# Maxout FFN behind cross attention on one core: transposes spread over the SyncE queue, deferred G copies, a last tile in two halves

## The chip, the core and the metric

The kernel runs on one core of a Trainium2 chip. The core has five engines with an instruction queue each: TensorE (PE, the matmuls; PEld are its weight loads), VectorE (DVE), ScalarE (ACT), GpSimd (POOL) and SyncE (SP, which here only issues DMAs). Instructions of one engine run in the order in which they were issued; engines wait for each other through semaphores. Matmuls write to PSUM, from which VectorE and ScalarE copy the results. The metric is the time of one execution on the device in microseconds (us), as a median over executions.

## What is computed

For each of 8 batches b and 8 heads h there are 512 rows x and 32 rows of state, 64 wide. Both read from each other by softmax attention, the results are put behind one another (544 rows for each batch, 4352 in all, the heads side by side to a width of 512), and a maxout FFN follows:

```python
scores = scale * np.matmul(x, state.transpose(0, 1, 3, 2))
a = np.exp(scores); a /= a.sum(-1, keepdims=True) + 1e-09     # over the 32 states
xread = np.matmul(a, state)
scores2 = scale * np.matmul(state, x.transpose(0, 1, 3, 2))
a2 = np.exp(scores2); a2 /= a2.sum(-1, keepdims=True) + 1e-09 # over the 512 rows
sread = np.matmul(a2, x)
t = np.concatenate([xread, sread], axis=2)                    # then (4352, 512)
h = np.maximum(np.maximum(t @ w1, t @ w2), t @ w3)            # d_ff = 768
out = h @ w_out
```

(The reference subtracts the row maximum before each exp.) Inputs and output are float32; the kernel computes in bf16 with float32 accumulation.

## The kernel before

**Algebra.** xread times w1, w2 or w3 is never computed by way of xread. `g_cols(b, ms)` multiplies the states of batch b with 128 columns of each of the three weights and so gives G, 256 rows (8 heads by 32 states) by 384 columns for each block m of 128 columns; `x_maxout(b, m)` multiplies the transposed softmax weights aT with G. d_ff = 768 makes six blocks m (NM = 6), each with 6 matmuls of 512 columns (three weights, two halves of the 256 states).

**One maxout (lines 264 to 279).** Three PSUM tiles `pw` are filled. ScalarE copies the first to `t0` in SBUF (line 275). If a copy is on the list `copies_due`, it is issued to ScalarE right behind that (line 277). VectorE takes the maximum of t0 and the second pw (line 278), and of that and the third (line 279), which gives one block of `ht`. The PSUM tag "pw" has four buffers, shared by pw, the output tiles `po`, the sread tile `psr` and the tiles of TensorE's transposes; a matmul that needs a buffer waits until the reader of what was in it before is done.

**G (lines 240 to 261).** Each block m is a PSUM tile `pg` of the tag "two", which has two buffers, also used by `scores`. The copy to G in SBUF is done by ScalarE: at once, or, where `defer` is True for this block, from `copies_due` inside the next maxout. `g_cols` first issues what is still on the list.

**For each batch.** `x_transpose` (TensorE) or `x_transpose_dma` (a DMA transpose on SP, line 163) gives xT, in two buffers; `scores` multiplies xT with the states and ScalarE takes exp into `e`; `softmax` sums, inverts (VectorE) and scales to `a` (GpSimd from batch 2 on); `a_transpose` or `a_transpose_dma` (SP, line 208) gives aT. `sread(b)` multiplies e with x, divides, and puts a small DMA transpose of the result (`sr`, 128 by 128, bf16, 32 KB) on the list `late` (line 230). `late_transposes()` issues what is on that list to SP. Its results, `ats`, are read only by `s_maxout`, in the last batch. `ffn_out(b, j)` multiplies 128 rows of ht with w_out (6 matmuls of 512 columns), ScalarE copies the 512 columns to `osb`, and every second tile they are stored.

**Order.** The program is unrolled and its order is written by hand. Lines 325 to 398 are a prologue: loads of x, states and weights (float32 to bf16, by GpSimd's DMA queue, lines 70 and 95), batches 0 and 1 interleaved, and the start of batch 2. Then batches b = 2 to 7 run in a loop (lines 401 to 428) of six `x_maxout(b, m)`, with other work in a slot behind each: after m = 0 the xT transpose of batch b+2 and the scores of n = b+1; then softmax, g_cols of b; after m = 2 the aT transpose of n; sread of n; after m = 4 `g_cols(n, (0, 1))`; after m = 5 `late_transposes`. `ffn_out(b-1, j)` stands behind m = 1, 2, 4, 5, in the last two cases ahead of the rest of its slot. In the last batch `s_maxout(m)` takes the place of the next batch's work. Lines 429 to 434 are the end: output tiles of batch 7 and of the sread rows, the last one with `split=True`.

Of the sread transposes, those of batches 0 to 3 are all issued at the first `late_transposes`, at the end of b = 2.

Of the kernel before, what the change touches and what calls it, by code (L numbers as in the profile page):

```python
# [8 lines left out]
F32 = mybir.dt.float32  # L9
# [6 lines left out]
def kernel(  # L16
# [14 lines left out]
    nc = tc.nc  # L31

    B, H, S, D = x.shape
    _, _, Ns, _ = state.shape
    HD = H * D
    SP = S + Ns
    T = B * SP
    d_model, d_ff = moe_w1.shape
# [3 lines left out]
    J = 4  # L42
    HS = H // 2
    NM = d_ff // 128
# [6 lines left out]
    work = ctx.enter_context(tc.tile_pool(name="work", bufs=2))  # L51
    pp = ctx.enter_context(tc.tile_pool(name="pp", bufs=2, space=bass.MemoryType.PSUM))
    ctx.enter_context(tc.manual_schedule())
    dve, act, pool = nc.vector.tensor_copy, nc.scalar.copy, nc.gpsimd.tensor_copy
# [34 lines left out]
    wout_sb = wpool.tile([128, NM, d_model], BF16, name="wout")  # L89
# [25 lines left out]
    def keep_busy(n):  # L115
        p = pp.tile([128, 1024], F32, tag="two", name="idle")
        for _ in range(n):
            nc.tensor.matmul(p[:, 0:512], zero[:, 0:128], zero, start=True, stop=True)  # L118


    def bd(b, h):
        return bds[b // 2][:, b % 2, h]
# [21 lines left out]
    xT, e, a, aT, G, ht, osb = {}, {}, {}, {}, {}, {}, {}  # L144

    def new(d, b, shape, name, bufs=2):
        d[b] = work.tile(shape, BF16, tag=name, bufs=bufs, name=name)
# [13 lines left out]
    def x_transpose_dma(b):  # L161
        new(xT, b, [128, H, 2, 128], "xT")
        nc.sync.dma_start_transpose(out=xT[b].rearrange("p h j t -> p (h j) t"), in_=x_sb[b][:, 0:XW])

    def scores(b, g0, g1):
        n = g1 - g0
        if g0 == 0:
            new(e, b, [128, J, 2, HS, Ns], "e")
        if n == 2:
            p = pp.tile([128, J, n, HS, Ns], F32, tag="two", name="ps")  # L170
        else:
            p = pp.tile([128, J, n, HS, Ns], F32, tag="pw", bufs=4, name="psh")
        for jj in range(2):
            for g in range(g0, g1):
                for s in range(HS):
                    h = 2 * s + g
                    nc.tensor.matmul(  # L177
                        p[:, 2 * jj:2 * jj + 2, g - g0, s, :], xT[b][:, h, jj, :],
                        bd(b, h).rearrange("p c n -> p (c n)"),
                        start=(g == g0 and s == 0 and (n == 2 or jj == 0)),  # L180
                        stop=(g == g1 - 1 and s == HS - 1), skip_group_check=True)
        nc.scalar.activation(out=e[b][:, :, g0:g1], in_=p, func=AF.Exp, scale=scale)  # L182

    def softmax(b, g0, g1, mul):
        n = g1 - g0
        if g0 == 0:
            new(a, b, [128, J, 2, HS, Ns], "a")
        den = work.tile([128, J, n, HS], F32, tag=f"den{n}", name="den")
        nc.vector.reduce_sum(out=den, in_=e[b][:, :, g0:g1], axis=AX.X)  # L189
        rden = work.tile([128, J, n, HS], F32, tag=f"rden{n}", name="rden")  # L190
        nc.vector.reciprocal(out=rden, in_=den)  # L191
        mul(  # L192
            out=a[b][:, :, g0:g1].rearrange("p j g s n -> p j (g s) n"),
            in0=e[b][:, :, g0:g1].rearrange("p j g s n -> p j (g s) n"),
            in1=rden.rearrange("p j g s -> p j (g s)").unsqueeze(3).to_broadcast((128, J, n * HS, Ns)))
# [40 lines left out]
    def flush_copies():  # L236
        while copies_due:
            copies_due.pop(0)()

    def g_cols(b, ms, copies=(nc.scalar.copy, nc.scalar.copy), defer=(False, False)):  # L240

        flush_copies()
        for m, copy, wait in zip(ms, copies, defer):
            if m == 0:
                new(G, b, [128, 2, NM * 384], "G", bufs=3)
            w, f = w_cols(m)
            p = pp.tile([128, 2, 512], F32, tag="two", name="pg")
            for s in range(HS):
                for g in range(2):
                    nc.tensor.matmul(  # L250
                        p[32 * s:32 * s + 32, g, 0:384].rearrange("p (i f) -> p i f", i=3),
                        bd(b, 2 * s + g)[64 * g:64 * g + 64, g, :], w[64 * g:64 * g + 64, s, :, f],
                        start=True, stop=True, tile_position=(64 * g, 32 * s))

            def place(m=m, p=p, copy=copy):
                copy(out=G[b][:, :, m * 384:(m + 1) * 384], in_=p[:, :, 0:384])  # L256

            if wait:
                copies_due.append(place)
            else:  # L260
                place()
# [19 lines left out]
    def x_maxout(b, m):  # L281
        maxout(b, m, 512,
               lambda i, k: G[b][:, k, m * 384 + i * 128:m * 384 + i * 128 + 128],
               lambda k: aT[b][:, :, k, :], 2)
# [6 lines left out]
    def ffn_out(b, j, split=False):  # L291
        if j == 0:
            osb[b] = work.tile([128, J, d_model], F32, tag="osb", name="osb")
        p = pp.tile([128, d_model], F32, tag="pw", bufs=4, name="po")
        for m in range(NM):
            nc.tensor.matmul(p, ht[b][:, m, j * 128:(j + 1) * 128], wout_sb[:, m, :],  # L296
                             start=(m == 0), stop=(m == NM - 1))
        o = osb[b]
        if split:
            halves = [work.tile([128, d_model // 2], F32, tag=f"oh{k}", bufs=1, name="oh") for k in range(2)]  # L300
            rows = out[b * SP:b * SP + S, :].rearrange("(p j) f -> p j f", j=J)[:, j, :]
            act(out=halves[0], in_=p[:, 0:256])
            nc.scalar.dma_start(out=rows[:, 0:256], in_=halves[0])
            dve(out=halves[1], in_=p[:, 256:512])
            nc.sync.dma_start(out=rows[:, 256:512], in_=halves[1])
            return
        act(out=o[:, j, :], in_=p)  # L307
        if b == "s":
            for k in range(4 * j, 4 * j + 4):
                r0 = k * SP + S  # L310
                (nc.sync if k % 4 < 2 else nc.gpsimd).dma_start(
                    out=out[r0:r0 + Ns, :], in_=o[32 * (k % 4):32 * (k % 4) + 32, j, :])
            return
        j0 = j if b == B - 1 and j >= 2 else j - 1
        if j == 1 or j == 3 or j0 == j:
            (nc.sync if b == B - 1 else nc.gpsimd).dma_start(  # L316
                out=out[b * SP:b * SP + S, :].rearrange("(p j) f -> p j f", j=J)[:, j0:j + 1, :],
                in_=o[:, j0:j + 1, :])


    def late_transposes():
        while late:
            late.pop(0)()
# [3 lines left out]
    states(0, act)  # L327
    for k in range(1, B // 2):
        nc.vector.memset(bds[k], 0.0)
    keep_busy(4)  # L330
    dve(out=x0_sb[0], in_=x0_f)
    x_transpose(0, 0, dve)
    x_transpose(0, 1, dve)
# [29 lines left out]
    sread(1)  # L363
    a_transpose(1, 0, act)
    a_transpose(1, 1, dve)
    g_cols(0, (2, 3))
    x_maxout(1, 0)
    x_maxout(0, 2)
    g_cols(1, (1, 2), defer=(False, True))
# [7 lines left out]
    x_maxout(0, 4)  # L377
    g_cols(1, (3, 4), defer=(False, True))
    x_maxout(1, 2)
    x_maxout(0, 5)  # L380
    scores(2, 0, 2)
    g_cols(1, (5,))
    x_maxout(1, 3)
    softmax(2, 0, 2, nc.gpsimd.tensor_mul)
    x_transpose_dma(3)
    ffn_out(0, 0)
    x_maxout(1, 4)
    g_cols(2, (0, 1))
    ffn_out(0, 1)
    load_x(4)  # L390
    for k in range(2, B // 2):
# [4 lines left out]
    sread(2)  # L396
    ffn_out(0, 2)
    ffn_out(0, 3)


    for b in range(2, B):
        n = b + 1
        slots = [[] for _ in range(NM)]
        if n < B:
            if n + 1 < B:
                slots[0].append(lambda: x_transpose_dma(n + 1))
            slots[0].append(lambda: scores(n, 0, 2))
            slots[1].append(lambda: softmax(n, 0, 2, nc.gpsimd.tensor_mul))
            slots[2].append(lambda: a_transpose_dma(n))
            if n % 2 and n + 1 < B:  # L410
                slots[2].append(lambda: states((n + 1) // 2, pool))
            slots[5].append(late_transposes)
            if n + 2 < B:
                slots[0].append(lambda: load_x(n + 2))
        else:
            for m in range(NM):
                slots[m].append(lambda m=m: s_maxout(m))
        slots[1].append(lambda: g_cols(b, (2, 3)))
        slots[2].append(lambda: g_cols(b, (4, 5)))
        if n < B:  # L420
            slots[3].append(lambda: sread(n))
            slots[4].append(lambda: g_cols(n, (0, 1)))
        for j, m in enumerate((1, 2, 4, 5)):
            slots[m].insert(0 if m > 2 else len(slots[m]), lambda j=j: ffn_out(b - 1, j))
        for m in range(NM):
            x_maxout(b, m)
            for f in slots[m]:
                f()
# [36 lines left out]
```

## Time and profile before

| | |
|---|---|
| median of 13 executions | 163.71 us (163.02 to 167.65) |
| the profiled execution | 163.06 us |
| its span, first to last instruction | 161.2 us |
| TensorE matmuls, busy | 148.6 us, 92% of the span |
| ScalarE, VectorE, GpSimd, busy | 96.9, 94.4, 51.0 us |
| GpSimd's DMA queue, SP's hardware queue | 49.2% and 22.6% of 16 DMA engines |
| granted TensorE clock | 1.00 |

The profile is of one execution, and times in it count from the first instruction. A row of the timeline has start, length, engine, line of the kernel, operation, what it writes and reads (out<-in), shapes and, behind an x, how many instructions were merged in it; in brackets the idle time of that engine before it and what ended it. A "q" behind an engine (SPq) means its queue: a DMA row there is the time that the queue took to issue the DMA, and it lands later. A matmul's length includes its way through the array, so that rows of unhindered matmuls overlap: six of 512 columns show 1.46, but the next ones start 1.29 to 1.31 after the first. A few matmul records are missing (x5 for six), and their time is not a wait.

### The profile page before, as it was taken

Reading aid. Unit: us, or ns where it says so; the run is one execution under the profiler, and the core shown is the slowest. Engines: PE = TensorE matmul, PEld = TensorE weight load, DVE = VectorE, ACT = ScalarE, POOL = GpSimd, SP = SyncE. Lnnn points to the kernel's source line nnn. Section 1 sums busy time; section 2 is a strip of 40 time slices with the busy share of each in tenths; the row PEclk is TensorE's granted clock in tenths of the full one; section 3 lists DMA queues with packets and bytes.
Section 4 is the critical chain, followed back from the end, with each engine's and each line's share of the span. In section 5 each row is a group of like instructions: output and inputs, shape, how many; then the busy total and the mean of one; then the engine's idle time right before and its main releaser. Section 6 shows DMA issues by size and latency. Waiting matters only on the chain.

```text
span 161.2 us, 3542 instructions
## 1 busy us (share of the span) xinstructions
PE 148.6 (92%) x1410; PEld 69.5 (43%) x1425; DVE 94.4 (59%) x161; ACT 96.9 (60%) x156; POOL 51.0 (32%) x72
## 2 busy tenths in 40 slices
PE   6775889999999999999799999999999999999990
PEld 2342433543554344443344344344434475566440
DVE  4788548586727665766366736673767484475201
ACT  3364577976748736974578287827782737633340
POOL 8859981000842417160204061411050100100140
PEclk9999999999999999999999999999999999999999
DMA  4999999959199993899995968070307030030374
GB/s 115 215 156 121 189 198 199 236 81 130 48 163 204 157 190 130 178 159 230 191 191 69 90 121 289 4 204 1 134 0 203 0 136 0 0 134 0 130 223 168
DMA packets 36720, 21.72 MB, mean 135 GB/s; under 512 B 21952, under 2 KB 34368, under 8 KB 36704
## 3 DMA queue, kind: packets, MB, share of 16 engines
q0 software_dynamic: 17216, 15.08, 49.2%
q1 hardware_dynamic: 19344, 6.29, 22.6%
q8 instruction: 11, 0.18, 0.5%
q10 hardware_dynamic: 144, 0.13, 0.2%
q14 instruction: 5, 0.04, 0.1%
HBM read 15.20 MB, written 8.91 MB: 150 GB/s over the span
## 4 chain that ended last, share of the span: by engine, by line
PE 61%; DMA 12%; DVE 9%; ACT 8%; issue 4%; POOL 4%; SPq 0%; DVEq 0%; POOLq 0%
PE pw L271 31%; PE po L296 21%; DMA aT<-a 5%; PE pg L250 4%; DMA w<-in_moe_w_dram 4%; DVE t L278 3%; ACT G L256 3%; ACT t L275 3%; DVE ht L279 3%; DMA x0f<-in_x_dram 2%; POOL a L192 2%; POOL w L95 2%; PE psr L222 2%; PE ps L177 2%; ACT osb L307 1%
## 5 line engine op out<-in xcount | busy, mean ns | idle before, releaser
L271 PE MATMUL pw<-aT,G 128*128 128x512 bf16 x288 | 71.2, 379 | 2.4 <-DMA aT<-a 1.0
L278 DVE TENSOR_TENSOR t<-t,pw 128x512 bf16<-128x512 bf16 (+1 forms) x54 | 35.1, 650 | 44.8 <-ACT t L275 39.5
L296 PE MATMUL po<-wout,ht 128*128 128x512 bf16 x189 | 48.0, 380 | 0.8
L271 PEld LDWEIGHTS <-G 128*128 128x128 bf16 x288 | 26.3, 98 | 35.7 <-issue 5.6
L256 ACT CAST G<-pg 128x768 bf16<-128x768 f32 x47 | 35.6, 805 | 9.2 <-PE pg L250 8.8
L275 ACT CAST t<-pw 128x512 bf16<-128x512 f32 (+1 forms) x54 | 30.6, 567 | 13.9 <-PE pw L271 13.1
L279 DVE TENSOR_TENSOR ht<-t,pw 128x512 bf16<-128x512 bf16 (+1 forms) x54 | 35.5, 658 | 5.6
L307 ACT COPY osb<-po 128x512 f32<-128x512 f32 x33 | 19.3, 586 | 22.6 <-PE po L296 22.2
L296 PEld LDWEIGHTS <-ht 128*128 128x128 bf16 x204 | 18.4, 97 | 25.1 <-issue 4.0
L192 POOL TENSOR_TENSOR a<-e,rden 128x1024 bf16<-128x1024 bf16 (+1 forms) x9 | 14.6, 1623 | 41.9 <-DVE rden L191 31.2
L316 POOL DMA_DIRECT2D out_dram<-osb x14 | 7.9, 567 | 46.4 <-ACT osb L307 29.9
L250 PE MATMUL pg<-w,bd 64*32 64x384 bf16 x384 | 12.8, 328 | 2.6 <-DMA w<-in_moe_w_dram 2.4
L189 DVE TENSOR_REDUCE den<-e 128x32 f32<-128x1024 bf16 (+1 forms) x10 | 9.9, 990 | 0.5 <-ACT e L182 0.5
L182 ACT ACTIVATE e<-ps 128x1024 bf16<-128x1024 f32 x6 | 6.1, 1024 | 5.3 <-PE ps L177 5.3
L95 POOL DMA_DIRECT2D w<-in_moe_w_dram x12 | 9.1, 775 | 0.0
L271 PE MATMUL pw<-ats,w 128*128 128x256 bf16 x72 | 8.8, 273 | 0.0
L250 PEld LDWEIGHTS <-bd 64*32 64x32 bf16 x384 | 3.6, 89 | 12.1 <-issue 12.1
L271 PEld LDWEIGHTS <-w 128*128 128x128 bf16 x72 | 7.0, 98 | 2.1
L140 POOL COPY bd<-stT 64x512 bf16<-64x512 bf16 x4 | 4.3, 1063 | 10.0 <-DMA stT<-st 9.9
L70 POOL DMA_DIRECT2D x<-in_x_dram x7 | 6.5, 922 | 0.0
L118 PE MATMUL idle<-zero 128*128 128x512 bf16 x13 | 5.1, 540 | 1.2 <-DVE zero L81 1.2
L177 PEld LDWEIGHTS <-xT 128*128 128x128 bf16 x128 | 4.7, 98 | 2.4 <-DVE xT L159 0.8
(43 smaller groups left out, 62.8 us busy)
## 6 DMA issues: line engine op xcount, KB each, us to landing
out_dram<-osb POOLq DMA_DIRECT2D x14, 512.0 KB, 3.6
x<-in_x_dram POOLq DMA_DIRECT2D x7, 512.0 KB, 8.4
w<-in_moe_w_dram POOLq DMA_DIRECT2D x6, 256.0 KB, 6.3
w<-in_moe_w_dram POOLq DMA_DIRECT2D x6, 128.0 KB, 6.8
wout<-in_moe_w_out_dram POOLq DMA_DIRECT2D x1, 768.0 KB, 11.6
x0f<-in_x_dram SPq DMA_DIRECT2D x1, 512.0 KB, 4.0
out_dram<-osb SPq DMA_DIRECT2D x1, 512.0 KB, 2.6
stf<-in_state_dram POOLq DMA_DIRECT2D x3, 128.0 KB, 10.9
```

The source lines that it names most:

```text
L95: nc.gpsimd.dma_start(out=w_sb[c][:, :, i, :], in_=w.rearrange("(kk p) f -> p kk f", p=128)[:, :, m0 * 128:m1 * 128])
L177: nc.tensor.matmul(p[:, 2 * jj:2 * jj + 2, g - g0, s, :], xT[b][:, h, jj, :], bd(b, h).rearrange("p c n -> p (c n)"), start=(g == g0 and s ...
L189: nc.vector.reduce_sum(out=den, in_=e[b][:, :, g0:g1], axis=AX.X)
L192: mul(out=a[b][:, :, g0:g1].rearrange("p j g s n -> p j (g s) n"), in0=e[b][:, :, g0:g1].rearrange("p j g s n -> p j (g s) n"), in1=rden.r ...
L250: nc.tensor.matmul(p[32 * s:32 * s + 32, g, 0:384].rearrange("p (i f) -> p i f", i=3), bd(b, 2 * s + g)[64 * g:64 * g + 64, g, :], w[64 * ...
L256: copy(out=G[b][:, :, m * 384:(m + 1) * 384], in_=p[:, :, 0:384])
L271: nc.tensor.matmul(p[:, 0:n], lhs(i, k), rhs(k), start=(k == 0), stop=(k == nk - 1))
L275: nc.scalar.copy(out=t0[:, 0:n], in_=pw[0][:, 0:n])
L278: nc.vector.tensor_max(t1[:, 0:n], t0[:, 0:n], pw[1][:, 0:n])
L279: nc.vector.tensor_max(ht[b][:, m, :], t1[:, 0:n], pw[2][:, 0:n])
L296: nc.tensor.matmul(p, ht[b][:, m, j * 128:(j + 1) * 128], wout_sb[:, m, :], start=(m == 0), stop=(m == NM - 1))
L307: act(out=o[:, j, :], in_=p)
```

## The change

Six edits, none of which changes what is computed.

1. `late_transposes()` is called at two more places in the prologue: before `x_transpose_dma(3)`, for batches 0 and 1, and before the loop, for batch 2. That of batch 3 remains where it was.
2. In the loop, `g_cols(n, (0, 1))` defers its second copy, into the `x_maxout(b, 5)` that follows.
3. In the prologue, `g_cols(0, (2, 3))` does the same, into `x_maxout(1, 0)`.
4. `scores(2, 0, 2)` moves ahead of `x_maxout(0, 5)`.
5. `keep_busy(4)` becomes `keep_busy(5)`: one more matmul on zeros before batch 0's transposes.
6. The last output tile. Before, six matmuls of 512 columns filled one PSUM tile, from which ScalarE and then VectorE copied a half each. Now each half of the columns has a PSUM tile and six matmuls of 256 columns of its own; VectorE copies the first half and SP stores it, ScalarE copies the second and its own queue stores it.

```diff
     def ffn_out(b, j, split=False):
         if j == 0:
             osb[b] = work.tile([128, J, d_model], F32, tag="osb", name="osb")
+        rows = None if b == "s" else out[b * SP:b * SP + S, :].rearrange("(p j) f -> p j f", j=J)
+        if split:
+            for k, (copy, eng) in enumerate(((dve, nc.sync), (act, nc.scalar))):
+                f = slice(256 * k, 256 * k + 256)
+                p = pp.tile([128, 256], F32, tag="pw", bufs=4, name="ph")
+                for m in range(NM):
+                    nc.tensor.matmul(p, ht[b][:, m, j * 128:(j + 1) * 128], wout_sb[:, m, f],
+                                     start=(m == 0), stop=(m == NM - 1))
+                oh = work.tile([128, 256], F32, tag=f"oh{k}", bufs=1, name="oh")
+                copy(out=oh, in_=p)
+                eng.dma_start(out=rows[:, j, f], in_=oh)
+            return
         p = pp.tile([128, d_model], F32, tag="pw", bufs=4, name="po")
...
-        if split:
-            halves = [work.tile([128, d_model // 2], F32, tag=f"oh{k}", bufs=1, name="oh") for k in range(2)]
-            rows = out[b * SP:b * SP + S, :].rearrange("(p j) f -> p j f", j=J)[:, j, :]
-            act(out=halves[0], in_=p[:, 0:256])
-            nc.scalar.dma_start(out=rows[:, 0:256], in_=halves[0])
-            dve(out=halves[1], in_=p[:, 256:512])
-            nc.sync.dma_start(out=rows[:, 256:512], in_=halves[1])
-            return
         act(out=o[:, j, :], in_=p)
...
-    keep_busy(4)
+    keep_busy(5)
     dve(out=x0_sb[0], in_=x0_f)
...
-    g_cols(0, (2, 3))
+    g_cols(0, (2, 3), defer=(False, True))
     x_maxout(1, 0)
     x_maxout(0, 2)
...
     x_maxout(1, 2)
+    scores(2, 0, 2)
     x_maxout(0, 5)
-    scores(2, 0, 2)
     g_cols(1, (5,))
     x_maxout(1, 3)
     softmax(2, 0, 2, nc.gpsimd.tensor_mul)
+    late_transposes()
     x_transpose_dma(3)
...
     ffn_out(0, 3)
+    late_transposes()
...
-            slots[4].append(lambda: g_cols(n, (0, 1)))
+            slots[4].append(lambda: g_cols(n, (0, 1), defer=(False, True)))
```

More of the change, by code (lines that the diff above doesn't have):

```diff
@@ L316, in ffn_out @@
             (nc.sync if b == B - 1 else nc.gpsimd).dma_start(
-                out=out[b * SP:b * SP + S, :].rearrange("(p j) f -> p j f", j=J)[:, j0:j + 1, :],
+                out=rows[:, j0:j + 1, :],
                 in_=o[:, j0:j + 1, :])
```

## The prediction, made before the changed kernel ran

> **What bounds the kernel now.** I read the page's chain of waits first (which engine it runs through), then TensorE's own waits, then the timeline at each place where TensorE's rows are longer than the work in them.
>
> ```profile
> PE 61%; DMA 12%; DVE 9%; ACT 8%; issue 4%; POOL 4%; SPq 0%; DVEq 0%; POOLq 0%
> ...
> PE pg L250 <- DMA w<-in_moe_w_dram: 2.4, 3, 1.4
> ...
> PE pw L271 <- DMA aT<-a: 1.0, 1, 1.0
> ```
>
> TensorE carries the chain, and the waits recorded on it are small. So only what TensorE still loses is to be had, plus the ends of the span. I find five places.
>
> First the SP queue and one late transpose (timeline of SP, then of TensorE; start, length, line, times merged):
>
> ```profile
> 58.76 5.48 SPq L230 DMA_TRANSPOSE ats<-sr  x4
> 64.35 6.35 SPq L163 DMA_TRANSPOSE xT<-x  x1
> 71.45 2.95 SPq L208 DMA_TRANSPOSE aT<-a  x1
> ...
> 75.87 1.47 PE L271 MATMUL pw<-aT,G 128*128 128x512 bf16 x6
> 77.18 1.46 PE L296 MATMUL po<-wout,ht 128*128 128x512 bf16 x6
> 79.62 1.24 PE L271 MATMUL pw<-aT,G 128*128 128x512 bf16 x5 [0.98 <-DMA aT<-a]
> ```
>
> Four sread transposes sit back to back on SP; the xT transpose of batch 5 stands behind them although its x landed at 56.75 (issued 48.35, 8.4 to landing). It then takes 11.4 us to land, beside the x load of 64.10, and the aT transpose of batch 4, behind it on the same queue, takes 8.0 where the other four take 3.3 to 5.8. TensorE normally starts the next six matmuls 1.31 after the last six (75.87 to 77.18); here it takes 2.44. Loss 1.13.
>
> Second, the turn from one batch to the next (timeline of ScalarE and TensorE; the same pattern at 62.48, 111.36 and 127.36):
>
> ```profile
> 92.92 1.51 ACT L256 CAST G<-pg 128x768 bf16<-128x768 f32 x2
> ...
> 94.30 0.62 ACT L275 CAST t<-pw 128x512 bf16<-128x512 f32 x1
> 94.94 0.69 DVE L278 TENSOR_TENSOR t<-t,pw 128x512 bf16<-128x512 bf16 x1 [2.58 <-ACT t L275]
> ...
> 95.38 1.69 PE L271 MATMUL pw<-aT,G 128*128 128x512 bf16 x6
> ...
> 95.73 0.69 DVE L279 TENSOR_TENSOR ht<-t,pw 128x512 bf16<-128x512 bf16 x1
> ...
> 96.48 0.10 PEld L271 LDWEIGHTS <-G 128*128 128x128 bf16 x1 [0.35 <-issue]
> ```
>
> Two G copies delay the maxout's first copy `t`, with it both maxima, and the last matmul pair, which needs the PSUM buffer that `ht` reads, starts only when `ht` is done (96.43). Six matmuls take 1.69 instead of 1.46: loss 0.23, four times.
>
> Third, the same pattern in the prologue, and the last tile:
>
> ```profile
> 21.35 3.33 PE L271 MATMUL pw<-aT,G 128*128 128x512 bf16 x12
> ...
> 157.48 0.37 ACT L302 COPY oh<-po 128x256 f32<-128x256 f32 x1 [0.71 <-PE po L296]
> 157.88 0.37 ACTq L303 DMA_DIRECT2D out_dram<-oh  x1
> 157.88 0.42 DVE L304 COPY oh<-po 128x256 f32<-128x256 f32 x1 [7.59 <-ACT oh L302]
> 158.34 0.35 SPq L305 DMA_DIRECT2D out_dram<-oh  x1
> ```
>
> Twelve unhindered matmuls take 2.76 (1.46 plus 1.30), so 0.57 is lost at 21.35. At the end VectorE's half starts when ScalarE's ends (both read one PSUM tile), and each store takes 1.9 to land.
>
> **The change, part by part.**
>
> *Second G copy behind the first maxout copy, in the loop.* The same ScalarE work in another order. `t` starts when the first G copy is done, at about 93.6 instead of 94.30 (pw is ready: TensorE started it at 92.78, and its first pair takes some 0.6 to be readable). `ht` then ends near 95.75, and the last pair would start at 96.24 (0.216 after the one of 96.02): the wait goes with some 0.45 to spare. The delayed copy runs from about 94.2 to 95.0, while ScalarE otherwise idles until 95.58; what it writes is read by the next batch's second maxout, at 97.4, and its PSUM buffer is wanted again only at 98.8. Gain 4 x 0.23 = **0.92**. Were the delayed copy not done by 95.5, the osb copy behind it would be late, and the po buffer is wanted again after 96: cover about 0.5.
>
> *sread transposes earlier.* ats of batches 0 and 1 can issue from 18.2 and 21.0 (their sr multiplies on VectorE end at 18.15 and 20.95); nothing stands ahead of them on SP, whose next transpose waits for x until 35.48. ats of batch 2 issues at 45.1, before the xT of 50.30. None of the three holds anything on SP. At 58.76 one is left, over at 60.0, and xT of batch 5 goes then, 4.3 earlier. From 60.6 to 62.6 the DMA engines' busy share is 0.18 and 0.03, and xT needs 4.3 (batch 7) or 4.9 (batch 3) when little else runs; it lands near 65, before most of the x load. The aT of 71.45 has neither beside it; with the 3.3 to 5.8 of the others it lands by 77.3, against 78.47 when TensorE comes for it. Gain **1.13**. Next late there would be the second-part wait, 0.23, also removed.
>
> The price: two transposes now run while weights stream in. In the Trainium skill, "DMA: Bandwidth & Descriptors", section "Issuing engines are not separate DMA queues", all queues end on the same 16 engines and interleave, so moving work to another time on SP is no free bandwidth. That speaks against this part. The trace's row: the x load of 64.10, beside a 16-block xT, took 9.9; the one of 80.08 took 6.8. That is 3.0/16 = 0.19 us for one block, and one ats is one block (alone, at 60.6, it is a busy share of 0.18 over 1 us). The same page's "Rules for kernel authors" (under 64 KB "mostly overhead"; its fit for GpSimd's DMAs has a fixed 2.0 us each) would give 2.0 for each, an estimate, if that overhead held up the load: one before the weights of 20.76, two before x of batch 2. I take the row, because an issue-to-landing time (2.3 here) is not occupation. On the path is the first one alone: TensorE waits at 20.90 for weights landing at 20.76. Cost **0.19** (0.1 to 2.0). The second delays x of batch 2 (landed 28.31) to 28.7; TensorE would then reach its transposes at 28.89 - 0.57 + 0.19 = 28.5 and wait 0.2, but the maxout after them already waits 0.3 for `ht` of the one before, so nothing is added.
>
> *Second G copy deferred in the prologue.* `t` at 22.05 instead of 22.71, so both waits inside the twelve matmuls go: gain **0.57** (0.3 to 0.6; the third buffer comes free only 0.1 before it is wanted). The wait at 27.07 for a G copy moves along with it.
>
> *Scores of batch 2 one maxout earlier.* 0.47 us of TensorE work only changes place. It fills a wait of 0.15 for `ht` near 33.1; but its exp (1.02 on ScalarE) now stands before the next maxout's `t`, which delays that `ht` by about 0.6 and could cost 0.35 at 36.9, while `t` of the maxout after it comes earlier and a wait of 0.18 near 38.8 goes. Taken as **0** (-0.3 to +0.3).
>
> *One more idle matmul.* Four took 1.74 at 4.00 and 1.03 at 8.36: TensorE's clock doubled in between, though the granted clock reads 1.00 in all windows. TensorE stands idle before 6.11, waiting for the x0 cast. The last of the four starts at 5.28; a slow fifth (0.43 apart) would run from 5.71 to 6.14, 0.03 late; a fast one is over by 5.9. The skill, "TensorE: Matmul & The Clock Gate", section "What's actually happening", says that the window which raises the clock runs freely, so the place of the switch differs between executions; one profile can't show that. **0** (up to 0.03 worse; where the switch falls late, some gain that I can't price).
>
> *Last tile in halves.* Twelve 256-column matmuls replace six of 512: the s maxout's twelve take 1.31 (128.88 to the next group at 130.19) against 1.29. The first half's copy and SP store run beside the second's matmuls. After the last matmul: ScalarE 0.37, 0.03 to the issue, 1.9 to land: 157.50 + 2.30 = 159.80 instead of 158.34 + 1.88 = 160.22. Gain **0.42**. Batch 7's third tile lands at 159.2 and stays hidden.
>
> Sum: 0.92 + 1.13 + 0.57 + 0.42 - 0.19 = 2.85 saved. The profiled execution took 163.06 (span 161.2): **160.2**. It lies 0.65 under the median of the runs shown; with that, **160.9**.
>
> **Rivals.** *The aT wait stays.* The x load or an output store (5.3 beside one at 104.75) may still slow it: only 0.3 of the 1.13 is got, 161.7. For it: batch 6's aT took 5.8 with no xT near. Against: 7.0 us from issue to need.
> *ScalarE stays the limit.* If the reordered copies only move the wait to the osb copy, 0.92 and 0.57 go: 162.4. Against: ScalarE is busy 60% and has the gap before 95.58.
> *Slower: the transposes block the weight stream.* The ats of 62.65 took 5.4 to land, beside stores, against 2.3 for its neighbours. Should each of the two early ones hold the load queue for those 3.1 extra, weights and x come 6 later in a stretch that is bound by them (DMA share 1.4), and 163.7 + 6.2 - 2.85 = 167. It decides from 1.4 us each. Against: the 0.19 above.
> *It does little.* Loads later in the prologue by 1, as much lost by the moved exp and in jitter of the landings: 163.
>
> **How the numbers follow.** Forecast 0.68, aT stays 0.12, ScalarE 0.08, little 0.06, slower 0.06. 0.5% of the median is 0.82, about what a measurement can tell from no change. The first two are faster beyond it, the third mostly, the fourth is "same". The forecast's own costs (the prologue's 0.3 either way, the weights' 0.1 to 0.5, the median's place) give 160.1 to 161.7; the range takes in the aT rival and most of the third: 159.7 to 162.4.
>
> **What would show it.** SP's row of ats at 58.8 down to one, xT near 60, aT of batch 4 landing before 77.5; rows "1.69 x6" turned to 1.46; batch-to-batch distance of the sread matmuls (now 16.0, 16.9, 16.0) 15.8 throughout; the row of twelve near 2.8; weights landing at 20.9 to 21.0 and not at 22; the last store within 2.4 of the last matmul. A weight landing over 1.4 later, or a new idle before a G read, would make me wrong.

## The result, and the profile after

The changed kernel takes 161.43 us (median of 11 executions, 160.32 to 163.31), the one before 163.55 in the same comparison (48 executions). The ratio is 0.987, 95% interval 0.984 to 0.990; it leaves out, on both sides, executions more than 1.5% above the fastest of their kernel. The forecast was 160.9, range 159.7 to 162.4. The profiled executions took 163.06 and 160.39, spans 161.2 and 158.6.

The chain of waits by engine (page of the changed kernel):

```profile
PE 78%; DMA 7%; POOL 6%; DVE 4%; issue 2%; ACT 1%; DVEq 0%; POOLq 0%
```

Before it was PE 61%, DMA 12%, DVE 9%, ACT 8%. The chain now runs along TensorE nearly without a break from 29 us on; the rest is loads in the prologue. TensorE's waits (total, times, longest):

```profile
PE pg L250 <- DMA w<-in_moe_w_dram: 2.3, 2, 1.2
...
PE pxt L156 <- DMA x<-in_x_dram: 0.5, 2, 0.3
```

`aT` no longer occurs among them. SP's timeline ahead of it:

```profile
59.84 1.18 SPq L230 DMA_TRANSPOSE ats<-sr  x1
61.20 3.14 SPq L163 DMA_TRANSPOSE xT<-x  x1
70.70 1.23 SPq L208 DMA_TRANSPOSE aT<-a  x1
```

One ats instead of four. xT of batch 5 goes at 61.2 instead of 64.35 and lands at 67.1 instead of 75.7; aT of batch 4 is issued in 1.2 instead of 2.95 and lands 4.5 later, at 75.2 (before: 8.0 later, at 79.48). TensorE (timeline) goes from batch to batch without a gap:

```profile
76.43 1.46 PE L308 MATMUL po<-wout,ht 128*128 128x512 bf16 x6
77.73 1.46 PE L271 MATMUL pw<-aT,G 128*128 128x512 bf16 x6
```

The last row's start comes 1.30 after the one before it; it was 2.44. At the turns (ScalarE's timeline, one turn):

```profile
91.02 0.81 ACT L256 CAST G<-pg 128x768 bf16<-128x768 f32 x1
91.72 0.60 ACT L275 CAST t<-pw 128x512 bf16<-128x512 f32 x1
92.19 0.83 ACT L256 CAST G<-pg 128x768 bf16<-128x768 f32 x1
93.69 0.59 ACT L311 COPY osb<-po 128x512 f32<-128x512 f32 x1 [0.67 <-PE po L308]
```

`t` stands between the two G copies, and ScalarE still idles 0.67 before the next osb copy, so that nothing behind is late. The six matmuls of this turn, at 93.49, show 1.46 and no longer 1.69. The prologue (TensorE's timeline):

```profile
20.86 0.52 PE L250 MATMUL pg<-w,bd 64*32 64x384 bf16 x16 [1.19 <-DMA w<-in_moe_w_dram]
21.31 2.76 PE L271 MATMUL pw<-aT,G 128*128 128x512 bf16 x12
...
28.65 1.07 PE L156 MATMUL pxt<-ident,x 128*128 128x128 bf16 x16 [0.20 <-DMA x<-in_x_dram]
...
36.48 1.46 PE L308 MATMUL po<-wout,ht 128*128 128x512 bf16 x5 [0.18 <-DVE ht L279]
```

Twelve matmuls take 2.76 instead of 3.33. A wait of 0.20 for x stands where there was one of 0.18 for `ht` (the next maxout starts at 29.55, before at 30.16), and there is the new wait for `ht` at 36.5. The end (timeline):

```profile
154.21 0.35 SPq L320 DMA_DIRECT2D out_dram<-osb  x1
154.25 0.42 DVE L303 COPY oh<-ph 128x256 f32<-128x256 f32 x1 [6.55 <-PE ph L300]
154.70 0.36 SPq L304 DMA_DIRECT2D out_dram<-oh  x1
154.91 0.37 ACT L303 COPY oh<-ph 128x256 f32<-128x256 f32 x1 [0.72 <-PE ph L300]
155.31 0.37 ACTq L304 DMA_DIRECT2D out_dram<-oh  x1
```

The copies no longer stand behind one another, but the halves land at 157.26 and 157.46, 2.56 and 2.15 after their issue; before, both took 1.9.

The 2.67 of the two spans can be booked by the starts of the sread matmuls (line 222) in the two traces, which stand at the same place of each batch:

| stretch | before | after | gain |
|---|---|---|---|
| start to batch 2's sread | 43.56 | 42.97 | 0.59 |
| batches 2 to 3 | 12.60 | 12.60 | 0.00 |
| 3 to 4 | 16.00 | 15.84 | 0.16 |
| 4 to 5 (holds the aT wait) | 16.90 | 15.76 | 1.14 |
| 5 to 6, 6 to 7 | 15.99, 15.99 | 15.76, 15.75 | 0.47 |
| batch 7's sread to the last matmul's end | 36.40 | 36.19 | 0.21 |
| last matmul's end to the span's end | 3.80 | 3.70 | 0.10 |

### The profile page after: what moved, and what is told of

Same layout as the page of the kernel before. It is cut to its first block, busy times and chain, and to the rows that moved or that the text cites. A ratio compares the mean times of both kernels' runs of the same rounds, so it can differ in the third digit from the quotient of the medians.

```text
span 158.6 us, 3552 instructions
## 1 busy us (share of the span) xinstructions
PE 147.5 (93%) x1416; PEld 70.2 (44%) x1432; DVE 94.3 (59%) x161; ACT 96.9 (61%) x156; POOL 51.0 (32%) x72
## 4 chain that ended last, share of the span: by engine, by line
PE 78%; DMA 7%; POOL 6%; DVE 4%; issue 2%; ACT 1%; DVEq 0%; POOLq 0%
PE pw L271 38%; PE po L308 27%; DMA x<-in_x_dram 6%; PE pg L250 6%; POOL w L95 4%; PE psr L222 2%; PE ps L177 2%; POOL a L192 2%; DMA stf<-in_state_dram 1%; PE pxt L156 1%; DVE bd L333 1%; DVE t L278 1%; PE ph L300 1%; DVE x L335 1%; DVE xT L159 0%
## 5 line engine op out<-in xcount | busy, mean ns | idle before, releaser
L271 PE MATMUL pw<-aT,G 128*128 128x512 bf16 x288 | 70.1, 380 | 0.7 <-DVE G L256 0.5
L308 PE MATMUL po<-wout,ht 128*128 128x512 bf16 x183 | 46.6, 380 | 1.0 <-DVE ht L279 0.2
L256 ACT CAST G<-pg 128x768 bf16<-128x768 f32 x47 | 36.3, 806 | 8.9 <-PE pg L250 8.5
L308 PEld LDWEIGHTS <-ht 128*128 128x128 bf16 x198 | 17.8, 98 | 24.7 <-issue 4.5
L250 PEld LDWEIGHTS <-bd 64*32 64x32 bf16 x384 | 3.6, 89 | 12.5 <-issue 12.1
L140 POOL COPY bd<-stT 64x512 bf16<-64x512 bf16 x4 | 4.3, 1064 | 11.7 <-DMA stT<-st 11.6
(45 smaller groups left out, 65.6 us busy)
```

What stands on the lines that cost most here:

```text
L250: nc.tensor.matmul(p[32 * s:32 * s + 32, g, 0:384].rearrange("p (i f) -> p i f", i=3), bd(b, 2 * s + g)[64 * g:64 * g + 64, g, :], w[64 * ...
L271: nc.tensor.matmul(p[:, 0:n], lhs(i, k), rhs(k), start=(k == 0), stop=(k == nk - 1))
```

## The experiments

**Theory:** the gains are those of the sum, each at its own place. **Rivals:** the aT wait has another cause than the place of the transposes; the gain of one edit is swallowed by that wait; transposes beside the weights cost more than they bring. For the end, the sum's 0.42 stood against the 0.10 that the changed kernel's trace had shown. First each of four edits alone, on the kernel before.

**Edit 1 alone.**

```diff
     softmax(2, 0, 2, nc.gpsimd.tensor_mul)
+    late_transposes()
     x_transpose_dma(3)
...
     ffn_out(0, 3)
+    late_transposes()
```

> Edit 1 alone on the kernel before. My sum: the aT transpose of batch 4 lands by 77.3 instead of 79.48, the loss of 1.13 at that turn goes, but the turn then shows the same 0.23 as the others (its G copies are not deferred here): span 161.2 - 0.90 = 160.3, up to 0.2 more if the weights of 20.76 land later. Rival 'weights blocked': weights land 3 later for each early transpose, span above 164. Rival 'aT stays': aT of batch 4 still takes 8 to land and the span stays at 161.2.

Median 162.69 against 163.60 (20 and 71 executions), ratio 0.999 (0.996 to 1.002), span 160.6. SP:

```profile
59.99 1.18 SPq L230 DMA_TRANSPOSE ats<-sr  x1
61.34 1.95 SPq L163 DMA_TRANSPOSE xT<-x  x1
71.71 1.23 SPq L208 DMA_TRANSPOSE aT<-a  x1
```

aT lands at 75.65 and the distance of batches 4 to 5 is 16.00, 0.90 under the profile before, as expected; it still holds the 0.23 of the turn. Batch 2's sread starts 0.26 later (43.82), with waits of 1.7 for x instead of 0.6; edit 3's trace, without early transposes, has the same 1.7, so this can't be put down to them. The weights of line 250 landed at 20.56: "weights blocked" falls. The medians differ by 0.9, but the ratio, which leaves out long executions, shows no gain. That this edit gains mainly where executions are long would fit both (see "The aT wait" below), and is not shown.

**Edit 2 alone.**

```diff
-            slots[4].append(lambda: g_cols(n, (0, 1)))
+            slots[4].append(lambda: g_cols(n, (0, 1), defer=(False, True)))
```

> Edit 2 alone on the kernel before. My sum: the rows of 1.69 for six matmuls at the turns become 1.46. Three of the four 0.23 reach the end (after the aT wait); the one at 62.48 comes before that wait and may only make TensorE wait longer for a landing that a queue of DMAs sets: span 161.2 - 0.69 = 160.5 (160.3 if the DMAs move along). Rival 'ScalarE stays the limit': rows of 1.69 stay or the next osb copy is late, span 161.2.

Median 162.33, ratio 0.991 (0.987 to 0.995), span 159.3. TensorE at one turn:

```profile
94.11 1.46 PE L271 MATMUL pw<-aT,G 128*128 128x512 bf16 x6
```

Every distance from batch 3 on is 15.75 or 15.76 instead of 16.0: the 0.23 is this copy's. That the distance of batches 4 to 5 is among them I had not expected: with all four ats in place and xT landing as late as 74.2, aT of batch 4 took 4.1 in this execution and nobody waited. Most of the 1.2 between the expected span and this one is that missing wait. So it is not fixed by the program; it differs between executions.

**Edit 3 alone.**

```diff
-    g_cols(0, (2, 3))
+    g_cols(0, (2, 3), defer=(False, True))
     x_maxout(1, 0)
```

> Edit 3 alone on the kernel before. My sum: the twelve matmuls at 21.35 take 2.76 instead of 3.33 and everything behind is 0.57 earlier: span 160.6. Rival 'swallowed': the aT transpose of batch 4 lands at 79.5 whatever TensorE does before, the gain is lost there as a longer wait, span 161.2. Between the two if the x loads that GpSimd issues move along only in part.

Median 163.08, ratio 0.9995 (0.996 to 1.003), span 160.7. TensorE:

```profile
20.66 0.52 PE L250 MATMUL pg<-w,bd 64*32 64x384 bf16 x16 [0.54 <-DMA w<-in_moe_w_dram]
21.11 2.76 PE L271 MATMUL pw<-aT,G 128*128 128x512 bf16 x12
```

The 0.57 at the twelve is gone, and from 20.66 to batch 2's sread (42.92) it takes 22.26 instead of 22.66. The rest of the 0.57 went to x of batch 2, which landed at 28.59 and was now waited for (0.39). The aT wait is there (batches 4 to 5: 16.99, before 16.90), 0.09 longer, so that little more was swallowed. The median's 0.5 fits; the ratio can't tell it from nothing.

**Edit 6 alone.**

```diff
+            for k, (copy, eng) in enumerate(((dve, nc.sync), (act, nc.scalar))):
...
+                p = pp.tile([128, 256], F32, tag="pw", bufs=4, name="ph")
...
-            act(out=halves[0], in_=p[:, 0:256])
...
-            dve(out=halves[1], in_=p[:, 256:512])
```

> Edit 6 alone on the kernel before. The term of my sum: the end 0.42 earlier, span 160.8, with a last store that takes 1.9 to land. What the trace of the changed kernel shows instead: the ScalarE half lands in 2.15 and the SP half in 2.56, behind the store of the tile before; then only 0.2 is gained, span 161.0. If the longer landing came from the other edits, it is 1.9 here.

Median 163.82, ratio 0.999 (0.994 to 1.004). The profiled execution is a long one (span 166.1), so the expected span says nothing. From the last matmul's end to the end of the span it has 3.67 (before 3.80), and the halves take 2.55 and 2.14 to land, as in the changed kernel: the longer landing belongs to this edit. The trace is worth more for another row. TensorE's timeline, then the windows (busy us of PE, PEld, DVE, ACT, POOL, with counts; granted clock; DMA share; GB/s):

```profile
82.01 2.72 PE L271 MATMUL pw<-aT,G 128*128 128x512 bf16 x6 [3.45 <-DMA aT<-a]
```

```profile
82.00:87.40 5.40, 5.39 (x27) 2.44 (x28) 1.38 (x3) 2.09 (x3) 0.00 (x0) 0.50 1.21 251
87.40:92.00 4.60, 4.60 (x49) 1.68 (x48) 3.91 (x6) 3.22 (x5) 1.40 (x1) 1.00 0.00 0
```

Here xT of batch 5, behind four ats, took 14.9 to land and aT of batch 4 landed at 81.87. TensorE waited 3.45, and then its granted clock was 0.50 for 5.4 us: six matmuls took 2.72. Batches 4 to 5 took 21.99, six more than the rest. So the aT wait can cost 0 (edit 2 alone), 0.9 (the kernel before) or 6.0 with one and the same order on SP.

**One swap on SP, without early transposes.** Does the place of xT decide?

```diff
                 slots[0].append(lambda: x_transpose_dma(n + 1))
+            if b > 2:
+                slots[0].append(late_transposes)
...
-            slots[5].append(late_transposes)
+            if n + 1 == B:
+                slots[5].append(late_transposes)
```

> The kernel before with one swap on SP: the sread transposes, still four in a row, are issued behind the xT transpose of batch 5 instead of ahead of it, none of them beside the weights. Theory 'place of xT': what counts is that xT of batch 5 goes at about 59 and lands before most of the x load; then aT of batch 4 lands by 76 without a wait, as in the run with edit 1 alone, and the median is 0.7 to 1.0 under that of before. Rival 'the number of transposes in that stretch': the four ats now lie between xT and aT, aT lands after 78 and TensorE waits as before.

Median 162.72 against 163.41, ratio 0.998 (0.995 to 1.001). SP:

```profile
59.25 1.93 SPq L163 DMA_TRANSPOSE xT<-x  x1
61.22 7.31 SPq L230 DMA_TRANSPOSE ats<-sr  x4
71.65 1.26 SPq L208 DMA_TRANSPOSE aT<-a  x1
```

xT landed at 63.5. But the four ats, now beside the x load of 64.3, landed as late as 74.7, aT took 7.9 again, and TensorE waited 0.9. In this execution the number of transposes in the stretch decided: with xT early but the four ats still there, the wait remained. The median gained 0.7 all the same, which the ratio can't tell from nothing.

**Price of a transpose beside the loads.**

```diff
     late = []
+    scratch = data.tile([128, 8, 128], BF16, name="scratch")
...
+        if b == 0:
+            for r in range(8):
+                late.append(lambda r=r: nc.sync.dma_start_transpose(
+                    out=scratch[:, r], in_=sr.rearrange("p g d -> p (g d)")))
```

> The changed kernel with eight more transposes of the same sr tile into a scratch tile that nobody reads, right behind the first early one: nine in place of one beside the weight and x loads. My price of 0.19 a block: the x load of batch 3, the last of that stream, lands 8 x 0.19 = 1.5 later than 35.7, at 37.2, and x of batch 2 (28.6) up to 1.5 later. Rival 'weights blocked': 3.1 a block, the stream ends some 25 later. Third way 'free': the trace of the changed kernel shows 320 small packets among 4750; if they only fill gaps, x of batch 3 lands within 0.4 of 35.7. A second look: the eight hold SP for up to 3 each, so that xT of batch 3 is issued late.

162.30 in one execution. SP:

```profile
18.34 11.93 SPq L235 DMA_TRANSPOSE scratch<-sr  x8
38.48 1.79 SPq L163 DMA_TRANSPOSE xT<-x  x1
```

The x load of batch 3 landed at 38.33 instead of 35.70: 2.6 for eight, 0.33 each, one execution against one. That is too little to set against my 0.19. From issue to landing this load took 15.47 here and 13.07 to 14.53 in the seven other traces with two early transposes, which makes 0.12 to 0.30 for each of the eight; the median of the seven is 13.43, that of six traces with none 12.70, which makes 0.37 for each of the two. So the price is 0.1 to 0.4, an estimate from these traces. "Free" falls, since none of the seven took so long. "Blocked" (3.1 each) is some ten times too dear, and the 2.0 that the prediction had as its upper end is out as well. xT of batch 3 went right behind its x, so SP did not hold it. TensorE's waits for weights were 3.2 instead of 2.3 and those for x 2.2 instead of 0.5, but the latter are 1.6 to 2.5 in four other traces with early transposes too.

**Edit 4 undone.**

```diff
-    scores(2, 0, 2)
     x_maxout(0, 5)
+    scores(2, 0, 2)
```

> The changed kernel with edit 4 undone. My sum: 0, the same median within 0.3. In the trace the wait of 0.34 for ht ahead of the first output tile (36.5) goes and waits of 0.15 and 0.18 for ht come back near 33 and 38.3; the sread matmuls of batch 3 start within 0.15 of the changed kernel's. Rival: the move is worth 0.3 or more, then they start that much later.

Median 160.97, of five executions only, ratio to before 0.988 (0.979 to 0.997). It lies 0.46 under the changed kernel's, more than the 0.3 expected, but the interval covers that kernel's 0.987. In its trace loads came late early on (2.5 waiting for x, 2.3 for weights) and the clock fell twice (last section), so absolute times can't be used. From the maxout behind batch 2's x transposes, where the clock was full again, to batch 2's sread it is 33.10 to 46.48, 13.38, against 13.42 with the move (29.55 to 42.97). The wait ahead of the first output tile is gone, and waits of 0.12 and 0.18 inside maxouts are back, as expected. In the trace the move is worth nothing, as booked.

**A fifth idle matmul, undone.**

```diff
-    keep_busy(5)
+    keep_busy(4)
```

> The changed kernel with four idle matmuls again. My term: 0, the transposes of batch 0 start at 6.11 in the trace with four as with five, and the median is that of the changed kernel within 0.5. Rival: the fifth keeps TensorE's clock up in executions where it rises late; then the median is 0.5 or more higher, with more executions whose mean granted clock is under 0.99.

Median 161.22 of eight, ratio to the kernel before 0.990 (0.986 to 0.995), which covers the changed kernel's. Batch 0's transposes start at 6.10 with four and at 6.11 with five, and all eight executions have a mean granted clock of 0.998 or more. No effect was found.

**The end.** Two variants of the changed kernel, one execution each.

```diff
-            (nc.sync if b == B - 1 else nc.gpsimd).dma_start(
+            (nc.sync if b == B - 1 and j < 2 else nc.gpsimd).dma_start(
```

> The changed kernel with the store of batch 7's third tile issued by GpSimd's queue instead of SP's. Theory 'same ring': the SP half (2.56 to land) waits for that store's packets in SP's own queue, and lands in 1.9 here; the ScalarE half, which shares the engines alone, in 1.9 to 2.1; the last landing comes 2.35 to 2.55 after the last matmul instead of 2.59. Rival 'the engines are shared': both halves still take 2.1 and more, 2.6 after the last matmul, or later if GpSimd's slower issue makes its own store the last.

161.05 us. The timeline of the end:

```profile
154.90 0.57 POOL L320 DMA_DIRECT2D out_dram<-osb  x1 [0.32 <-ACT osb L311]
155.13 0.35 SPq L304 DMA_DIRECT2D out_dram<-oh  x1
```

With the large store off SP's queue the SP half still takes 2.60 to land, the ScalarE half 2.43, the last lands 2.87 after the last matmul (2.59 before the move). So the SP half is slow without that store in SP's own queue as well. That all stores share the engines, whichever queue issues them, fits, but is not shown by this: GpSimd issued the large store 0.3 nearer to the last matmul, and small stores of SP's were still landing until 156.22.

```diff
-    ffn_out("s", 0)
-    ffn_out("s", 1)
-    ffn_out(B - 1, 2)
+    ffn_out(B - 1, 2)
+    ffn_out("s", 0)
+    ffn_out("s", 1)
```

> The changed kernel with batch 7's third tile ahead of the two sread tiles, so that ahead of the halves stand four small stores, half of them on SP. Theory 'same ring': SP still has 128 KB ahead of its half, which lands in 2.2 to 2.5; the last landing 2.45 to 2.6 after the last matmul. If only one large store in flight was the cause, 2.35. If the four issues (0.4 each on SP) hold the SP half up, it is the last and the end is later than 2.6.

162.45 us. Behind four small stores the halves take 3.43 and 3.37, the last landing comes 3.8 after the last matmul. Only the third expectation allowed more than 2.6, and its reason fails: the SP half goes only 0.4 later than in the changed kernel and is not the last; most of the loss is in the landing.

**Two candidates.** The first fills TensorE's wait at 20.86.

```diff
-    g_cols(0, (2, 3), defer=(False, True))
     x_maxout(1, 0)
+    g_cols(0, (2, 3), defer=(False, True))
     x_maxout(0, 2)
...
+    x_maxout(0, 4)
     states(1, act)
     x_transpose(2, 0, dve)
     x_transpose(2, 1, act)
-    x_maxout(0, 4)
```

> A candidate: the changed kernel with x_maxout(1, 0) ahead of g_cols(0, (2, 3)), and x_maxout(0, 4) ahead of the state and x transposes of batch 2. In the changed kernel TensorE is idle 1.2 at 20.86 for weights, with a maxout behind it that doesn't need them, and 0.35 at 28.65 for x of batch 2. If both waits are filled and no other comes, the sread matmuls of batch 3 start 1.3 earlier and the span is 157.3. If ScalarE or VectorE, which then have two maxouts close together, become the limit, or the weights of the next chunk, it is 0.3 to 0.8 only.

Median 161.92, ratio to before 0.992 (0.990 to 0.995), where the changed kernel has 0.987. The wait for weights near 20.9 is gone, but waits of 1.0 in all for G copies and 0.5 for an aT copy come in its place, and batch 2's sread starts at 44.85, not earlier. The reason named beforehand for a smaller gain fits: with two maxouts close together TensorE now waits for ScalarE's copies.

The second issues the two early transposes where few loads run.

```diff
-    late_transposes()
     x_transpose_dma(3)
+    late_transposes()
```

> The changed kernel with the two early sread transposes behind the xT transpose of batch 3, where few loads run, instead of beside the weights and x. By the runs so far one block lengthens the x loads by 0.3 to 0.4: the x load of batch 2 takes 8.2 to 8.9 here instead of 9.2 to 9.4, that of batch 3 12.5 to 13.2 instead of 13.4 to 13.8. On the path nothing or up to 0.35, since the maxout behind the x transposes waits for ht as well: median 160.9 to 161.4. Rival: nine tenths of the gain hung on their early place, then the aT wait is back.

Median 161.08 of four, ratio to before 0.989 (0.981 to 0.997). The x loads of batches 2 and 3 take 8.7 and 12.5, as in kernels without early transposes, and no aT wait shows. It keeps the gain without the price, but can't be told from the changed kernel in time. None of the versions tried is clearly better than the changed kernel.

## Why the prediction was right, point by point

**The turns.** Predicted 4 x 0.23. Shown by edit 2 alone: each distance falls by 0.24. In the changed kernel the four turns gave 0.84 instead of 0.92. The first gave 0.16: its scores start 0.09 late, at 63.27, as GpSimd's copy of their states ends (63.22).

**The aT wait.** Predicted 1.13, with aT landing by 77.3; it landed at 75.2 and the stretch is 1.14 shorter. The way there was slower than the step had it: xT of batch 5 went at 61.2, not 60.0, and landed at 67.1, not near 65. The place was right, but one profile had made a fixed 1.13 of something that varies; that the number fits to 0.01 is luck. In five traces without edit 1 the wait cost 0 (edit 2 alone), 0.8 (the swap), 0.9, 1.0 and 6.0; in the nine with edit 1 there is none. In those five the last transpose ahead of this aT on SP landed at 74.2, 74.7, 75.7, 76.5 and 79.5, in the same order; in the nine at 65.6 to 68.0. So in these traces the wait goes with the landing of what stands ahead on SP. Why that comes at 74 in one execution and at 79 in another was not settled: xT early is not enough (the swap), and neither it nor three ats fewer is needed (edit 2 alone).

The times fit. In the comparison of the four edits, 15 of the 131 executions of the kernel before and of edits 2, 3 and 6 alone lasted over 3 us more than their kernel's median; none of the 68 of the six kernels with edit 1 that ran more than once did (of the kernel before in the other comparisons, 4 of 98). That all 15 had a long aT wait is not shown: one of them has a profile, and the trace of edit 4 undone, 2.9 over its median, is long by other waits, for x and weights.

**The price of the early transposes.** Predicted 0.19 on the path. What one block costs lies between 0.1 and 0.4, so the size was not refuted. But in the changed kernel's profile it cost nothing there: the weights for line 250 landed at 20.72 (before 20.76). The first transpose, issued at 17.47, landed only at 23.7, and 18 of its some 160 packets had started by 20.72. What went slower was x of batch 2 (9.2 to landing instead of 8.6; 8.8 to 10.2 in the seven traces with early transposes, 8.2 to 8.9 in the six without); TensorE's wait for it lay under the wait for `ht`, as the step said.

**The prologue's deferral.** Predicted 0.57, measured 0.57 at the twelve matmuls and 0.59 at batch 2's sread.

**The scores, the idle matmul.** Predicted 0 and 0; both were undone and neither showed an effect. The trade in the step, a new wait at 36.5 for two old ones, is in the trace.

**The last tile.** Predicted 0.42, measured 0.19 to the last landing and 0.10 to the span's end. The term that failed is "1.9 to land": it came from two stores issued when the tile before was nearly stored. In the changed kernel the SP half goes 0.49 behind that tile's store instead of 1.55 and takes 2.56. The ScalarE half is as far behind it as before (1.10), but 0.61 behind the SP half, where it had been the first of the two, and takes 2.15. How much each of these neighbours costs was not separated; that the queue shared with the store before was at fault was tried, and moving that store away did not help.

**The median.** The sum was 2.85, the two profiled executions differ by 2.67, the medians by 2.1. That the profiles come so near is partly luck: the end gave 0.32 too little and the turns 0.08, the price of 0.19 did not show, and the other two terms are within 0.02. I carried the profile's 0.65 under its median over to the new kernel; the changed kernel's profiled execution lies 1.04 under its own. The start of batch 2's sread alone ranges from 42.9 to 46.5 over the traces, with the landings of x and weights, and a single profile can't place that.

## What to carry to other kernels

A wait for a DMA that is seen in one profile is one draw: look at how far ahead of its use the transfer is issued, against the spread of its landings, and price it as a distribution. When a copy is only moved behind another on the same engine, the gain can be read off exactly from the buffer that the next matmul waits for, here 0.24 at each turn with that edit alone. A store at the very end gains less than the time by which it is issued earlier when the stores before it are still moving, here 0.19 for 0.46.

## What I had not expected of the hardware

In edit 6's trace a wait of TensorE of 3.45 us was followed by 5.4 us at half its clock (six matmuls in 2.72 instead of 1.46), so that 6.0 were lost, some 2.5 of them to the clock. In the trace of edit 4 undone the clock also fell behind shorter waits. The page has the granted clock in tenths, in 40 slices of 4.05 us; below it are TensorE's waits (total, times, longest):

```profile
PEclk9995999699999999999999999999999999999999
```

```profile
PE pg L250 <- DMA w<-in_moe_w_dram: 2.6, 2, 2.3
PE pxt L156 <- DMA x<-in_x_dram: 2.5, 1, 2.5
```

The wait for x ended at 11.7, and the clock was 0.50 from 12.3 to 15.7; the one for weights ended at 28.6, and it was 0.50 from 29.4 to 32.7. Waits of up to 1.7 us (edit 6's trace, for weights) had no such effect.

And the same transpose, 32 KB and 128 by 128, lands in 2.3 us when little else runs and in 4.8 to 8.3 beside the loads of the prologue.
